# Second network's float64 weights: half-size units through a ring of four, paced behind the gate activations

## The chip, the cores and the metric

The kernel runs on one core of one Trainium2 chip. The metric is the device time of one execution in microseconds (us), the median over runs. Engines are named as in the profile: PE (TensorE's matmuls), PEld (its weight loads, which overlap them), DVE (VectorE), ACT (ScalarE), POOL (GpSimd) and SP (the engine whose queue issues nearly all DMAs here).

## What is computed

An attention between 512 tokens and 32 state rows per batch and head, whose output goes through two feed-forward networks. Inputs `x` and `state` are float32; the weights `w_gate`, `w_val`, `w_out`, `w_in2` (`moe2_w_in`) and `w_out2` (`moe2_w_out`) are float64 and are turned into float32 on the chip.

```python
# attention: x (8, 8, 512, 64), state (8, 8, 32, 64)
scores = scale * np.matmul(x, state.transpose(0, 1, 3, 2))      # softmax -> a
xread = np.matmul(a, state)
scores2 = scale * np.matmul(state, x.transpose(0, 1, 3, 2))     # softmax -> a2
sread = np.matmul(a2, x)
x = concat([xread, sread])            # as rows: (4352, 512)
# first network, d_ff 1536
g = x @ w_gate
x = (g * (1 / (1 + np.exp(-g))) * (x @ w_val)) @ w_out
# second network, d_ff 2048
h = x @ w_in
out = (np.maximum(h, 0) + alpha * np.minimum(h, 0)) @ w_out
```

## The kernel before, in words

The first network goes over eight blocks of 512 tokens (one batch each, `blocks[0]` to `blocks[7]`, called blocks 0 to 7 here) and then one of the 256 state rows. Blocks 0 and 1 run together with the conversion of the first network's weights. Blocks 2 to 7 go through `ffn1`, which is a loop over `f` = 0 to 11, slices of 128 of the 1536 hidden columns. In each `f`, PE makes the gate product (six matmuls) and ACT applies Silu to it (`gate`, tile `s`, from bank `g`); PE makes the value product and DVE multiplies the two (`value`, bank `v`); ACT and DVE split the result in a rounded part and a rest (`split`, tile `h`: ACT writes the first, `sub_lo` on DVE the second); and PE projects the slice before, `project(f - 1)`, twelve matmuls into four banks `acc`. At `f` = 0 `finish` ends the block before: its last projection, copies of the four banks to `xo` (two on ACT, two on DVE), and stores to `x2d`.

`slots` holds what else is done in a block, by `f` and one of three places: 0 behind the gate, 1 behind value and split, 2 behind the projection. There stand the products of the state with the weights (`state_times_w`, tiles `sw`, at place 2 of each even `f`), the attention of the next block's batch (`scores` at `f` = 3 and 7, with two PSUM banks `aux` that they share with `state_times_w`), and the preparation of the second network's weights.

That preparation takes the float64 words in units. `Unit.load` is one DMA of 1 MB of words into a tile `raw`; `Unit.act` is two ACT instructions over the tile's high and low words (L267, L268, 128 x 1024 each); `Unit.bits` is two DVE instructions and a POOL addition for one half of the unit, which leave float32 words in `m32`; `uses` hands them to `take`, which puts sums, splits (`sp`) and stores into the list `later`, of which `one_later` does one or two at place 2. `Stream.step` does the acts of unit d every second step, the bits of a half of unit d - 1, and the uses of a half of unit d - 2, and loads one unit ahead. 16 units (8 of `w_in2`, 8 of `w_out2`, in turn) take 8 steps a block, at `f` = 1, 2, 4, 5, 7, 8, 10, 11 of blocks 2 to 6; block 7 only empties `later`.

In this part PE's order is the order of the program. The order on DVE, ACT, POOL and SP is made by a scheduler when the kernel is built, from the program's dependences; `tc.issue_after(i)` tells it to place what is issued under it behind instruction i. Each engine, and SP's queue of DMAs, then takes its instructions strictly in that order: one that waits holds up all behind it. From the block of state rows on the order of all engines is written out by hand.

Of the kernel before, what the change touches and what calls it, by code (L numbers as in the profile page):

```python
# [25 lines left out]
def attention_and_two_ffns(ctx: ExitStack, tc: tile.TileContext, x, state, w_gate, w_val,  # L26
# [7 lines left out]
    P = 128  # L34
# [9 lines left out]
    XT = 2  # L44
    EARLY = 3

    const = ctx.enter_context(tc.tile_pool(name="const", bufs=1))
# [195 lines left out]
    def words(w, r0, r1, c0, c1):  # L243
        return w.bitcast(I32)[r0 * P:r1 * P, 2 * c0:2 * c1].rearrange("(a p) n -> p a n", p=P)

    class Unit:
# [39 lines left out]
        def uses(self, i):  # L286
            if self.take:
                self.take(i, self.m[i].bitcast(F32))

    class Stream:  # L290

# [47 lines left out]

    units1, units2 = [], []  # L340
    for j in range(NJ1):
# [76 lines left out]
    def one_later():  # L418
        for _ in range(2 if len(later) > 3 else 1):
            if later:  # L420
                later.pop(0)()

    for j in range(NJ2):
        units2.append(Unit([words(w_in2, 0, NPAIR, 2 * P * j, 2 * P * (j + 1))], take=take_w2(j)))
        units2.append(Unit([words(w_out2, 2 * j, 2 * j + 2, 0, DM)], take=take_wo2(j)))
    stream1, stream2 = Stream(units1, 3), Stream(units2, 1)

# [31 lines left out]
    class Block:  # L459
# [21 lines left out]
        def gate(self, f, idle=0):  # L481

            if self.keep:
                if f % 2 == 0:
                    self.kept = t4([P, 2, S], F32, "p")
                self.p[f] = self.kept[:, f % 2]
            else:
                self.p[f] = t2([P, S], F32, "s")[:, :self.n]
            return nc.scalar.activation(self.p[f], self.product(f, 0, self.banks(f)[0], idle), AF.Silu)

# [61 lines left out]
    with tc.manual_schedule(engines={mybir.EngineType.PE}):  # L552
# [67 lines left out]
        def ffn1_slots(b):  # L620
            slots = {}

            def put(f, i, th):
                slots.setdefault((f, i), []).append(th)

            for j in range(1, NJ1):
                put(2 * j - 2, 2, lambda j=j: state_times_w(b, j))
            if b < B - 1:
                for f in range(NF1):
                    if f % 3 != 0:  # L630
                        put(f, 1, stream2.step)
                    put(f, 2, one_later)
            if b == B - 1:
                for f in range(NF1):
                    put(f, 2, one_later)
                put(0, 2, lambda: nc.sync.dma_start(alpha_sb, alpha.rearrange("(k p) -> p k", p=P)))
# [110 lines left out]
        todo.setdefault((1, 10), []).append(lambda: state_times_w(XT, 0))  # L747
        todo.setdefault((1, 8), []).append(lambda: stream2.load(1))
        for b in range(XT):
# [517 lines left out]
```

## Time and profile before

| | us |
|---|---|
| median of 3 runs | 1426.53 (1426.47 to 1428.33) |
| the profiled execution | 1423.65 |
| its span, from first to last instruction | 1421.6 |
| PE busy | 1366.7 (96%) |
| DVE busy | 1031.0 (73%) |
| ACT busy | 826.8 (58%) |
| POOL busy | 554.9 (39%) |

The span has three parts: blocks 0 and 1 with the first weights (up to 203 us), blocks 2 to 7 (203 to 685 us), and the state rows and the second network (from 685 us). PE is the engine to look at: where another engine is idle and PE is not, nothing is lost. Idle time of PE, and time in which its clock is granted at half speed, is what the span can lose.

### The profile page before, as it was taken

What the parts mean: (1) busy time and instruction counts of PE and PEld (TensorE: products, weight loads), DVE (VectorE), ACT (ScalarE), POOL (GpSimd) and SP (SyncE); (2) the same over time, 40 slices, a digit from 0 to 9 for tenths busy, and PEclk for the clock granted to TensorE, in tenths of its full rate; (3) what the DMA queues carried; (4) which work ended last, traced back from release to release, by engine and by line L of the source; (5) the groups of instructions that cost most, each with busy time, mean ns of one, the idle gap of its engine ahead of it and who ended that gap; (6) DMA issues with size and microseconds to landing.
All of it is one profiled execution on the core that took longest, in us unless ns stands there. A gap on an engine that the chain in (4) does not pass through costs nothing.

```text
span 1421.6 us, 20610 instructions
## 1 busy us (share of the span) xinstructions
PE 1366.7 (96%) x7238; PEld 1069.2 (75%) x7238; DVE 1031.0 (73%) x1593; ACT 826.8 (58%) x1408; POOL 554.9 (39%) x422
## 2 busy tenths in 40 slices
PE   6899999989899999999999999999999999999997
PEld 3566777767676676777887888878888888888886
DVE  6878545769687887634566688888897899878651
ACT  6666443565555554433456767666677667666642
POOL 4432111313232332100005665666665656656611
PEclk8999999999999999999999999999999999999999
DMA  9442232495857856310415688679877897786792
GB/s 298 154 157 46 81 104 49 140 243 175 254 149 224 236 173 182 113 45 1 156 53 206 186 279 282 209 185 317 308 234 222 268 317 244 207 245 233 264 311 102
DMA packets 274223, 271.91 MB, mean 191 GB/s; under 512 B 133704, under 2 KB 198216, under 8 KB 273096
## 3 DMA queue, kind: packets, MB, share of 16 engines
q1 hardware_dynamic: 271976, 270.21, 61.6%
q8 instruction: 57, 0.93, 0.3%
q10 hardware_dynamic: 2144, 0.39, 0.2%
q14 instruction: 46, 0.38, 0.1%
HBM read 206.05 MB, written 64.49 MB: 190 GB/s over the span
## 4 chain that ended last, share of the span: by engine, by line
PE 75%; DVE 9%; DMA 5%; ACT 3%; issue 3%; POOL 2%; SPq 2%; ACTq 0%; DVEq 0%; POOLq 0%
PE acc L1036 17%; PE acc L516 16%; PE v L476 8%; PE g L476 8%; PE v L924 7%; PE g L924 5%; PE aux L924 5%; PE aux L442 3%; DVE h L83 2%; DMA raw<-in_moe_w_out_dram 2%; PE acc L1106 2%; DMA wo<-ws2d 1%; DVE sw L83 1%; POOL u L936 1%; PE aux L162 1%
## 5 line engine op out<-in xcount | busy, mean ns | idle before, releaser
L1036 PE MATMUL acc<-h,wo 128*128 128x512 f32 x1344 | 341.5, 390 | 2.5 <-ACT sum L77 1.3
L516 PE MATMUL acc<-h,wp 128*128 128x512 f32 (+1 forms) x1296 | 300.2, 382 | 11.1 <-DVE h L83 8.2
L1036 PEld LDWEIGHTS acc<-h,wo 128*128 128x128 f32 x1344 | 251.2, 188 | 56.4 <-ACT sum L77 2.6
L516 PEld LDWEIGHTS acc<-h,wp 128*128 128x128 f32 x1296 | 235.6, 190 | 63.2 <-DVE h L83 10.6
L893 POOL TENSOR_TENSOR u<-u,m 128x512 f32<-128x512 f32 x96 | 128.6, 1340 | 346.1 <-ACT m L892 312.9
L83 DVE TENSOR_TENSOR h<-u,h 128x512 fp32r<-128x512 f32 x160 | 147.4, 937 | 23.1 <-ACT h L77 22.7
L476 PE MATMUL g<-a,sw 128*128 128x512 f32 x576 | 153.8, 401 | 3.6 <-ACT h L77 1.7
L476 PE MATMUL v<-a,sw 128*128 128x512 f32 x576 | 153.3, 402 | 0.5 <-DVE p L492 0.4
L77 ACT ACTIVATE h<-u 128x512 fp32r<-128x512 f32 x160 | 100.3, 630 | 88.4 <-POOL u L936 87.1
L476 PEld LDWEIGHTS g<-a,sw 128*128 128x128 f32 x576 | 103.8, 188 | 62.6 <-issue 24.3
L924 PE MATMUL v<-x,w 128*128 128x512 f32 x576 | 146.4, 389 | 0.1
L1047 DVE TENSOR_TENSOR sum<-acc,sum 128x512 f32<-128x512 f32 x184 | 125.5, 683 | 24.8 <-PE acc L1036 24.4
L476 PEld LDWEIGHTS v<-a,sw 128*128 128x128 f32 x576 | 106.4, 190 | 33.8 <-issue 9.5
L924 PEld LDWEIGHTS v<-x,w 128*128 128x128 f32 x576 | 107.8, 188 | 22.6 <-DVE u L932 0.5
L284 POOL TENSOR_TENSOR m<-m,raw 128x512 int32<-128x512 int32 x44 | 61.8, 1407 | 153.9 <-DVE m L276 95.5
L83 DVE TENSOR_TENSOR h<-h,h 128x512 fp32r<-128x512 f32 (+1 forms) x80 | 78.7, 984 | 43.1 <-ACT h L77 42.3
L936 POOL TENSOR_TENSOR u<-u,u 128x512 f32<-128x512 f32 x64 | 105.4, 1647 | 5.0
L83 DVE TENSOR_TENSOR sw<-aux,sw 128x512 fp32r<-128x512 f32 x96 | 62.6, 682 | 56.1 <-ACT sw L77 56.1
L77 ACT ACTIVATE h<-s 128x512 fp32r<-128x512 f32 (+1 forms) x84 | 50.3, 598 | 90.5 <-DVE s L492 90.2
L492 DVE TENSOR_TENSOR s<-s,v 128x512 f32<-128x512 f32 (+1 forms) x79 | 52.0, 659 | 67.9 <-PE v L476 54.3
L892 ACT ACTIVATE m<-m,alpha_sb 128x512 f32<-128x512 f32 (+1 forms) x144 | 99.2, 689 | 0.0
L924 PE MATMUL g<-x,w 128*128 128x512 f32 x384 | 97.6, 390 | 0.8 <-ACT h L891 0.8
(155 smaller groups left out, 2120.9 us busy)
## 6 DMA issues: line engine op xcount, KB each, us to landing
wo<-ws2d SPq DMA_DIRECT2D x224, 256.0 KB, 5.2
w<-w2d SPq DMA_DIRECT2D x104, 512.0 KB, 5.5
w2d<-sp SPq DMA_DIRECT2D x32, 512.0 KB, 3.9
raw<-in_moe_w_out_dram SPq DMA_DIRECT2D x14, 1024.0 KB, 5.2
x2r<-x2d SPq DMA_DIRECT2D x25, 512.0 KB, 6.2
w<-w2d SPq DMA_DIRECT2D x48, 256.0 KB, 5.5
x2d<-xo SPq DMA_DIRECT2D x32, 256.0 KB, 3.0
raw<-in_moe_w_in_dram SPq DMA_DIRECT2D x8, 1024.0 KB, 6.2
```

Source lines behind the costliest of these rows:

```text
L77: return nc.scalar.activation(o, i, AF.Copy)
L83: (eng or nc.vector).tensor_tensor(out=o, in0=src, in1=hi.bitcast(F32), op=ALU.subtract)
L284: nc.gpsimd.tensor_tensor(out=m, in0=m, in1=lo, op=ALU.add)
L476: nc.tensor.matmul(o[:, :self.n], self.lhs(f, k, a, which), self.rhs(k, c), start=(i == 0), stop=(i == last))
L492: return nc.vector.tensor_tensor(out=self.p[f], in0=self.p[f], in1=self.product(f, 1, self.banks(f)[1]), op=ALU.mult)
L516: nc.tensor.matmul(self.acc[e][:, :self.n], wo1[f // 2][:, f % 2, a, e * P:(e + 1) * P], t[:, c, :self.n], start=(self.n == S and f == 0 a ...
L892: nc.scalar.activation(n, n, AF.Copy, scale=alpha_sb[:, f:f + 1])
L893: nc.gpsimd.tensor_tensor(out=out, in0=out, in1=n, op=ALU.add)
L924: nc.tensor.matmul(o, w[:, a, q], x[k][:, q, e], start=start and n == 0, stop=stop and n == 5, skip_group_check=True)
L936: nc.gpsimd.tensor_tensor(out=o, in0=x0, in1=x1, op=ALU.subtract)
L1036: nc.tensor.matmul(o, w[:, f, a, e], h[:, q], start=first and i == 0, stop=i == 5, skip_group_check=True)
L1047: nc.vector.tensor_tensor(out=r, in0=o, in1=r, op=ALU.add)
```

## The change

The 16 units of the second network become 32 halves. Each half has a DMA of 0.5 MB of its own, into a quarter of two fixed `raw` tiles (a ring of four, the half `n` takes place `n` mod 4), and two acts of 128 x 512. A step does the acts of half k, the bits of half k - 1 and the uses of half k - 2, and loads half k + 2, which takes the place of half k - 2. There are six steps a block, at `f` = 1, 2, 5, 6, 9, 10, now over blocks 2 to 7. A step stands under `tc.issue_after` of the block's newest gate activation. What the acts, bits and uses compute is as before.

```diff
+    STEPS2 = (1, 2, 5, 6, 9, 10)
...
+    class Half:
+        ring = []
+
+        def __init__(self, src, n, take):
+            self.src, self.n, self.take = src, n, take
+
+        def load(self):
+            if len(Half.ring) < 2:
+                Half.ring.append(t8([P, 2 * HALF, 2], I32, "raw"))
+            self.raw = Half.ring[self.n // 2 % 2][:, HALF * (self.n % 2):HALF * (self.n % 2 + 1)]
+            nc.sync.dma_start(self.raw.rearrange("p (a n) t -> p a (n t)", a=self.src.shape[1]), self.src)
+
+        def act(self):
+            lo, hi = self.raw[:, :, 0], self.raw[:, :, 1]
+            nc.scalar.activation(hi.bitcast(F32), hi.bitcast(F32), AF.Copy, scale=REBIAS)
+            nc.scalar.activation(lo, lo.bitcast(U32), AF.Copy, scale=2.0 ** -29)
+
+        def bits(self):
+            m = self.m = t2([P, HALF], I32, "m32")
...
+            nc.gpsimd.tensor_tensor(out=m, in0=m, in1=lo, op=ALU.add)
+
+        def uses(self):
+            self.take(self.n % 2, self.m.bitcast(F32))
+
+    class Halves:
...
+        def step(self):
+            h = lambda q: [self.halves[q]] if 0 <= q < len(self.halves) else []
+            for u in h(self.k):
+                u.act()
+            for u in h(self.k - 1):
+                u.bits()
+            for u in h(self.k - 2):
+                u.uses()
+            self.k += 1
+            self.load(self.k + 2)
...
-        units2.append(Unit([words(w_in2, 0, NPAIR, 2 * P * j, 2 * P * (j + 1))], take=take_w2(j)))
-        units2.append(Unit([words(w_out2, 2 * j, 2 * j + 2, 0, DM)], take=take_wo2(j)))
-    stream1, stream2 = Stream(units1, 3), Stream(units2, 1)
+        for src, take in ((words(w_in2, 0, NPAIR, 2 * P * j, 2 * P * (j + 1)), take_w2(j)),
+                          (words(w_out2, 2 * j, 2 * j + 2, 0, DM), take_wo2(j))):
+            n = src.shape[1] // 2
+            for i in range(2):
+                halves2.append(Half(src[:, n * i:n * (i + 1)], len(halves2), take))
+    stream1, stream2 = Stream(units1, 3), Halves(halves2)
...
-            return nc.scalar.activation(self.p[f], self.product(f, 0, self.banks(f)[0], idle), AF.Silu)
+            self.gated = nc.scalar.activation(self.p[f], self.product(f, 0, self.banks(f)[0], idle), AF.Silu)
+            return self.gated
...
+            def paced():
+                with tc.issue_after(blocks[b].gated.ins):
+                    stream2.step()
+
             for j in range(1, NJ1):
                 put(2 * j - 2, 2, lambda j=j: state_times_w(b, j))
-            if b < B - 1:
-                for f in range(NF1):
-                    if f % 3 != 0:
-                        put(f, 1, stream2.step)
-                    put(f, 2, one_later)
+            for f in range(NF1):
+                if f in STEPS2:
+                    put(f, 1, paced)
+                put(f, 2, one_later)
             if b == B - 1:
-                for f in range(NF1):
-                    put(f, 2, one_later)
...
-        todo.setdefault((1, 8), []).append(lambda: stream2.load(1))
+        todo.setdefault((1, 8), []).append(lambda: stream2.load(2))
```

PE's order of instructions does not change. On the other engines it changes in blocks 2 to 7 and shortly ahead of them, and nowhere from the block of state rows on. Three places follow; the numbers behind a name are buffers'.

ACT, block 3, from the Silu of `f` = 1 to the `sw` copies behind `f` = 2. Before (`h_2666` is the split of `f` = 0, `h_2731` of `f` = 1, `h_2787` of `f` = 2, `raw_2734` the acts of a unit):

```order
L489 ACTIVATE s_2714<-g_2715 128x512
L77 ACTIVATE h_2666<-s_2626 128x512
L77 ACTIVATE sw_2693<-aux_2694 128x512
L77 ACTIVATE sw_2699<-aux_2700 128x512
L77 ACTIVATE h_2731<-s_2714 128x512
L77 ACTIVATE sp_2758<-sc_2709 128x512 x2
L489 ACTIVATE s_2766<-g_2767 128x512
L77 ACTIVATE h_2787<-s_2766 128x512
L267 ACTIVATE raw_2734<-raw_2734 128x1024
L268 ACTIVATE raw_2734<-raw_2734 128x1024
L77 ACTIVATE sw_2806<-aux_2807 128x512
L77 ACTIVATE sw_2812<-aux_2813 128x512
```

The same stretch after, from the Silu of `f` = 1:

```order
L547 ACTIVATE s_2722<-g_2723 128x512
L307 ACTIVATE raw_1801<-raw_1801 128x512
L308 ACTIVATE raw_1801<-raw_1801 128x512
L78 ACTIVATE h_2739<-s_2722 128x512
L547 ACTIVATE s_2765<-g_2766 128x512
L307 ACTIVATE raw_1801<-raw_1801 128x512
L308 ACTIVATE raw_1801<-raw_1801 128x512
L78 ACTIVATE h_2786<-s_2765 128x512
L78 ACTIVATE sw_2808<-aux_2809 128x512
L78 ACTIVATE sw_2814<-aux_2815 128x512
```

The acts have moved from between split and `sw` to right behind each Silu, ahead of that slice's split, and the split of `f` = 0 no longer stands behind the Silu of `f` = 1.

DVE, block 3, `f` = 0 and 1. Before (`s` is the multiplication of `value`, `s_2626` of `f` = 0 and `s_2714` of `f` = 1; `h_2666` is the rest of the split of `f` = 0):

```order
L492 TENSOR_TENSOR s_2626<-s_2626,v_2658 128x512
L80 COPY xo_2681<-acc_370_1996 128x512
L80 COPY xo_2687<-acc_372_1998 128x512
L492 TENSOR_TENSOR s_2714<-s_2714,v_2723 128x512
L83 TENSOR_TENSOR h_2666<-s_2626,h_2666 128x512
L83 TENSOR_TENSOR sw_2693<-aux_2694,sw_2693 128x512
```

After (`s_2631` and `h_2671` are of `f` = 0, `s_2722` of `f` = 1):

```order
L551 TENSOR_TENSOR s_2631<-s_2631,v_2663 128x512
L84 TENSOR_TENSOR h_2671<-s_2631,h_2671 128x512
L84 TENSOR_TENSOR sw_2698<-aux_2699,sw_2698 128x512
L81 COPY xo_2686<-acc_370_1997 128x512
L81 COPY xo_2692<-acc_372_1999 128x512
L84 TENSOR_TENSOR sw_2704<-aux_2705,sw_2704 128x512
L84 TENSOR_TENSOR sp_2715<-sc_2626,sp_2714 128x512 x2
L551 TENSOR_TENSOR s_2722<-s_2722,v_2731 128x512
```

The split's rest for `f` = 0 now stands right behind its own multiplication and not behind that of `f` = 1.

SP's queue of DMAs at the start of block 3. Before (`raw_2734` is the unit whose acts stand in the first piece above):

```order
L126 DMA xq_2651<-in_x_dram 32x16x32 x4
L139 DMA xn_2656<-in_x_dram 128x4x256
L525 DMA x2d_89<-xo_2681 128x512
L525 DMA x2d_89<-xo_2684 128x512
L525 DMA x2d_89<-xo_2687 128x512
L525 DMA x2d_89<-xo_2690 128x512
L258 DMA raw_2734<-in_moe_w_out_dram 128x2x1024
L407 DMA ws2d_108<-sp_2758 128x4x256
```

After:

```order
L584 DMA x2d_89<-xo_2695 128x512
L461 DMA ws2d_108<-sp_2714 128x4x256
L461 DMA ws2d_108<-sp_2715 128x4x256
L303 DMA raw_1799<-in_moe_w_in_dram 128x2x512
L418 DMA w2d_101<-sp_2829 1024x1x128
L419 DMA w2d_101<-sp_2830 1024x1x128
L303 DMA raw_1801<-in_moe_w_out_dram 128x1024
L140 DMA xn_2912<-in_x_dram 128x4x256
```

The loads still stand behind the stores of the block before, but these two are of halves whose acts come at `f` = 5 and 6, where the 1 MB load was of the unit whose acts come at `f` = 2.

## Rows read from the trace of the kernel before

**Rows 1.** The page's head and busy times: busy us, share of the span, instructions.

```profile
span 1421.6 us, 20610 instructions
PE 1366.7 (96%) x7238; PEld 1069.2 (75%) x7238; DVE 1031.0 (73%) x1593; ACT 826.8 (58%) x1408; POOL 554.9 (39%) x422
```

**Rows 2.** Windows, blocks 2 to 7: stretch, length, busy by engine, clock, DMA, GB/s.

```profile
202.62:280.74 78.12, 78.12 (x466) 56.56 (x465) 50.52 (x96) 37.55 (x63) 19.04 (x16) 1.00 0.31 77
280.74:365.12 84.38, 80.32 (x466) 57.26 (x465) 65.05 (x128) 48.07 (x82) 24.58 (x22) 0.98 0.73 209
365.12:449.32 84.20, 80.40 (x466) 57.61 (x465) 65.58 (x128) 48.12 (x82) 25.24 (x22) 0.98 0.73 209
449.32:531.69 82.37, 78.75 (x466) 56.48 (x464) 64.72 (x124) 48.28 (x82) 24.61 (x22) 1.00 0.73 214
531.69:612.23 80.54, 78.49 (x466) 56.47 (x464) 52.78 (x98) 36.16 (x64) 13.44 (x12) 1.00 0.48 133
612.23:684.79 72.56, 72.56 (x377) 55.20 (x376) 27.78 (x40) 24.10 (x40) 0.00 (x0) 1.00 0.07 22
```

**Rows 3.** Timeline of PE, block 3: start, us, instruction, count [idle before, releaser].

```profile
291.77 2.79 PE L516 MATMUL acc<-h,wp 128*128 128x512 f32 x11 [1.13 <-DVE h L83]
...
305.42 1.61 PE L162 MATMUL aux<-xt,bd 128*64 128x512 f32 x4 [2.82 <-DVE sw L83]
306.96 2.69 PE L476 MATMUL v<-a,sw 128*128 128x512 f32 x6
```

**Rows 4.** Timeline of PE, the same waits in blocks 5 and 6.

```profile
460.35 2.83 PE L516 MATMUL acc<-h,wp 128*128 128x512 f32 x11 [1.13 <-DVE h L83]
...
473.60 1.08 PE L162 MATMUL aux<-xt,bd 128*64 128x512 f32 x4 [2.38 <-DVE sw L83]
...
554.37 1.08 PE L162 MATMUL aux<-xt,bd 128*64 128x512 f32 x4 [0.97 <-DVE sw L83]
```

**Rows 5.** Windows, behind the second wait of block 3, columns as above.

```profile
306.00:308.00 2.00, 2.00 (x7) 0.85 (x4) 2.00 (x4) 0.83 (x3) 1.57 (x2) 0.50 0.45 147
```

**Rows 6.** Timeline of ACT, block 3, ahead of the second wait.

```profile
302.04 1.14 ACT L267 ACTIVATE raw<-raw 128x1024 f32<-128x1024 f32 x1 [2.25 <-DMA raw<-in_moe_w_out_dram]
...
304.06 1.07 ACT L77 ACTIVATE sw<-aux 128x512 fp32r<-128x512 f32 x2
```

**Rows 7.** Timeline of DVE, block 3.

```profile
290.43 0.69 DVE L492 TENSOR_TENSOR s<-s,v 128x512 f32<-128x512 f32 x1 [4.04 <-PE v L476]
291.03 0.68 DVE L83 TENSOR_TENSOR h<-s,h 128x512 fp32r<-128x512 f32 x1
...
304.67 1.29 DVE L83 TENSOR_TENSOR sw<-aux,sw 128x512 fp32r<-128x512 f32 x2 [2.42 <-ACT sw L77]
```

**Rows 8.** SP's timeline in block 3, and landing times of the loads of raw.

```profile
293.87 0.75 SPq L258 DMA_DIRECT2D raw<-in_moe_w_out_dram  x1
...
DMA to landing us min/median/max: 5.0/5.7/8.1
```

**Rows 9.** Timeline of ACT, block 2, splits of f = 1 and 2.

```profile
213.03 0.63 ACT L77 ACTIVATE h<-s 128x512 fp32r<-128x512 f32 x1 [1.19 <-DVE s L492]
...
218.47 0.63 ACT L77 ACTIVATE h<-s 128x512 fp32r<-128x512 f32 x1 [1.49 <-DVE s L492]
```

**Rows 10.** Groups of ACT in blocks 2 to 6: busy, mean ns | idle, releasers.

```profile
L267 ACT ACTIVATE raw<-raw 128x1024 f32<-128x1024 f32 x13 | 14.9, 1144 | 19.0 <-DMA raw<-in_moe_w_out_dram 12.3 <-DMA raw<-in_moe_w_in_dram 5.7 <-POOL sp L83 0.9
L268 ACT ACTIVATE raw<-raw 128x1024 int32<-128x1024 uint32 x13 | 14.5, 1119 | 0.0
...
L77 ACT ACTIVATE sp<-m 128x512 fp32r<-128x512 f32 x16 | 9.1, 617 | 0.0
```

**Rows 11.** Timeline of DVE and of PE, block 2, f = 1 and 2.

```profile
213.70 0.69 DVE L83 TENSOR_TENSOR h<-s,h 128x512 fp32r<-128x512 f32 x1 [0.70 <-ACT h L77]
...
217.48 1.75 PE L516 MATMUL acc<-h,wp 128*128 128x512 f32 x7
```

**Rows 12.** Timeline of PE, behind block 7.

```profile
700.42 1.65 PE L516 MATMUL acc<-h,wp 128*128 128x256 f32 x11 [2.53 <-DVE h L83]
```

More of the change, by code (lines that the diff above doesn't have):

```diff
@@ L288, in uses, with __init__, load @@
                 self.take(i, self.m[i].bitcast(F32))
+    class Half:
[13 more added lines that the diff above has]
+            m = self.m = t2([P, HALF], I32, "m32")
+            lo, hi = self.raw[:, :, 0], self.raw[:, :, 1]
+            nc.vector.tensor_scalar(out=m, in0=hi, scalar1=0x0FFFFFFF, scalar2=3, op0=ALU.bitwise_and,
+                                    op1=ALU.logical_shift_left)
+            nc.vector.scalar_tensor_tensor(out=m, in0=hi, scalar=-0x80000000, in1=m, op0=ALU.bitwise_and,
+                                           op1=ALU.bitwise_or)
+            nc.gpsimd.tensor_tensor(out=m, in0=m, in1=lo, op=ALU.add)
+        def uses(self):
+            self.take(self.n % 2, self.m.bitcast(F32))
+    class Halves:
+        def __init__(self, halves):
+            self.halves, self.k, self.loaded = halves, 0, 0
+        def load(self, n):
+            while self.loaded < min(n, len(self.halves)):
+                self.halves[self.loaded].load()
+                self.loaded += 1
+        def step(self):
[8 more added lines that the diff above has]
+            self.load(self.k + 2)
     class Stream:
@@ L338, in unit_o @@
                     banks=("acc0", "acc1") if j < EARLY else ("g", "v"))
-    units1, units2 = [], []
+    units1 = []
     for j in range(NJ1):
@@ L421, in one_later @@
                 later.pop(0)()
+    halves2 = []
     for j in range(NJ2):
-        units2.append(Unit([words(w_in2, 0, NPAIR, 2 * P * j, 2 * P * (j + 1))], take=take_w2(j)))
-        units2.append(Unit([words(w_out2, 2 * j, 2 * j + 2, 0, DM)], take=take_wo2(j)))
-    stream1, stream2 = Stream(units1, 3), Stream(units2, 1)
+        for src, take in ((words(w_in2, 0, NPAIR, 2 * P * j, 2 * P * (j + 1)), take_w2(j)),
[4 more added lines that the diff above has]
+    stream1, stream2 = Stream(units1, 3), Halves(halves2)
     class StateTimesW:
```

## The prediction

> **What bounds the kernel now.** I read the page's busy times first: PE is busy for 1366.7 us of a span of 1421.6 [rows 1], so a change can only give back PE's idle time and time at a lower clock. The windows by block come next. Blocks 2 to 6 have the same PE work, 466 matmuls each, yet block 2 takes 78.12 us with PE busy throughout, and blocks 3, 4, 5 and 6 take 84.38, 84.20, 82.37 and 80.54 [rows 2]. So block 2 shows what a block costs when nothing holds PE up, and the four others lie 6.26, 6.08, 4.25 and 2.42 us above it, 19.01 us together. PE's idle time in them (length less PE busy) is 4.06, 3.80, 3.62 and 2.05, 13.53 us together; the other 5.48 us is PE time that got longer.
>
> PE's timeline tells where. In block 3 PE waits twice: 1.13 us in the projection of f = 0 for DVE's `h` (line 83), and 2.82 us ahead of `scores` at f = 3 for DVE's `sw` [rows 3]. The same two stand in blocks 4 and 5, and block 6 still waits 0.97 us for `sw` at `scores` [rows 4]. Behind the 2.82 us the granted clock is 0.50 of full speed, 1.2 GHz in place of 2.4, in the window from 306 to 308 us [rows 5], and six matmuls of `v` take 2.69 us there [rows 3]. That is where most of the longer PE time of blocks 3 and 4 comes from, whose mean clock is 0.98 against 1.00 in the other blocks [rows 2].
>
> The timelines of the other engines tell why. At f = 3 `scores` needs a PSUM bank that `sw` holds until ACT and DVE have read it. ACT comes to `sw` at 304.06 only, because the acts of a unit stand ahead of it in ACT's order and wait 2.25 us for their DMA [rows 6]; DVE then waits 2.42 us for ACT [rows 7]. The load was issued at 293.87, behind the block's stores in SP's queue, and landings took up to 8.1 us [rows 8]. At f = 1 it is order alone: DVE writes the rest of `h` of f = 0 at 291.03, behind the multiplication of f = 1, which waited until 290.43 for PE's `v` [rows 7]; in ACT's order, too, that split stands behind the Silu of f = 1.
>
> **The change part by part.** PE's work and order are the same, so each part is a question of whether it leaves PE without a wait.
>
> The f = 1 wait. The new order has the rest of `h` of f = 0 right behind its own multiplication, as in block 2, where PE did not wait. The wait goes in blocks 3 to 6.
>
> The f = 3 wait. Three things go at once. No act stands any more between the split of f = 2 and `sw`; the acts at f = 1 and 2 are of halves that were loaded at f = 9 and 10 of the block before; and a load at f = 1 now serves f = 5. A slice of f is about 78.12 / 12 = 6.5 us, so a load has at least three slices, 19.5 us, and mostly four, 26 us. A whole unit landed within 5.0 to 8.1 us [rows 8]; half of it should not take longer. The ACT waits for raw, 12.3 + 5.7 us in blocks 2 to 6 [rows 10], should be near 0.
>
> What is added on ACT. 32 halves with two acts each take the place of 16 units with two of 1144 and 1119 ns [rows 10], 36.2 us. A 128x512 act costs between half of these, 0.57 us, and the 617 ns of another copy of that shape [rows 10]; I take 0.6 us, so 38.4 us, 2.2 us more on an engine that is busy for 47 to 57% of these blocks. What matters is their place, between the Silu and the split. There ACT sat idle for 1.19 and 1.49 us in block 2, waiting for DVE [rows 9]. Two acts fill 1.14 to 1.23 us of that, so a split is late by 0.04 us at most where the data is there. The cover behind that is wide: in block 2 the rest of `h` of f = 1 started at 213.70 and PE began to project that slice at 217.48 [rows 11], 3.1 us after the 0.69 us of DVE's instruction. I cost it at 0. If that cover were gone, each us of lateness would be a us of PE.
>
> What is added on DVE, POOL and SP. The same bits, additions and stores, over six blocks in place of five. DVE is busy for 65 of 84 us in block 3 [rows 2] and gets six halves a block in place of eight. Behind the split of f = 2 it has its bits and four small sums ahead of `sw`, so `sw` there can still be late by DVE alone. The bounds for that are 0, as in block 2, and the 0.97 us of block 6 [rows 4] in each of four blocks, 3.9 us; I take 1 us in all, near block 2, since the work ahead of it shrinks. Each SP load now waits for the POOL addition of the half whose place it takes, which belongs to the step before; stores and loads for attention are queued behind it, with slices of time left, so 0.
>
> Block 7 had no steps and 27.78 us of DVE and 24.10 us of ACT in 72.56 [rows 2]. It gets four with acts and the list behind them. There an early weight split for the state rows on ACT, placed in front of the split of f = 5, now waits for the last half's POOL addition to free its buffer. I count about 1 us for that wait and a cover of about 2 us until the projection of f = 5: 0, at worst one wait like the 2.53 us behind block 7 [rows 12].
>
> Behind block 7 all orders are as before, and the wait there, on a reload of the first blocks' results, stays.
>
> **The sum.** 1423.65 us (profiled execution) - 19.01 (blocks 3 to 6 down to block 2) + 1 (left of f = 3) = 1405.6 us. The median of the runs, 1426.53, is 1.002 of the profiled execution, so 1405.6 becomes 1408.5 us.
>
> The Trainium skill speaks against the smaller loads: its page "DMA: Bandwidth & Descriptors", section Measured, says to batch DMAs to 1 MiB or more, and its section on the anatomy of one DMA puts a fixed 2.0 us on each. By that an estimate from the page is 16 x 2.0 = 32 us of DMA time more, and no run here has shown a half yet. Were that exposed in full, the sum would be 1440 us; it is not by the lead above.
>
> **The rivals.** First, loads that come late after all. If a half isn't there when its act comes, ACT stands with the split and `sw` behind it, and PE pays what block 3 paid at f = 3: 6.26 less about 1.5 for the f = 1 wait with its restart, about 4.7 us. There are 15 pairs of acts behind the first pair. Five such pairs cost 23.5 us and make it slower than before; all cost 70, 1423.65 - 19 + 70 = 1475 us, 1478 as a median. For it: SP's loads wait for POOL, and SP is in order. Against it: 19.5 us and more of lead for 8.1 at most. This is the place where the page's rule would bite. Chance 7%.
>
> Second, a smaller gain: the waits shrink but stay. DVE as the last to come at `scores` would leave 0.97 us in each of four blocks, and if the restart or a reordered `h` at f = 1 leaves 1.5 us each, 4 x 2.5 = 10 us stays; a new wait in block 7 would be about 4 us with half a clock period behind it. Gain 8 to 15 us, 1411.5 to 1418.5. For it: block 6 shows a wait for `sw` although no acts stand there any more (the 16 units' are done by the end of block 5), and the new order puts DVE's sums ahead of `sw`. Against it: block 2 has the same engines and no wait. Chance 20%.
>
> Third, no change: the waits go to other places of the same blocks, for instance to the projections, since a split stands behind two acts in every paced slice. That needs 17 us of new waits, 0.5 us in each of 34 steps. Against it: the cover of 3.1 us [rows 11]. Chance 6%. That the change doesn't do what it says can be left out, since the new orders stand in front of the reader.
>
> **How the numbers follow.** The forecast, 1408.5 us (1405 to 1411.5), has 67%; smaller gain 20%; no change 6%; slower 7%. The range reaches from 1405, which is all of the 19.01 and 2.5 us more, to 1418, nearly the end of the smaller gain, and leaves out the 13% of the last two and some edges. A measurement of this kernel can tell about 0.2% (2.9 us) from no change. Faster by more than that 0.87, within it 0.06, slower 0.07.
>
> **What would show it.** Right: blocks 3 to 6 at about 78 us each; no PE wait for `h` at f = 1 and under 1 us for `sw` at f = 3; granted clock 1.00 through blocks 2 to 7; ACT's waits for the DMA of raw gone; block 7 still near 72.6 us. Wrong: ACT waits for raw in front of a split, or PE waits at projections of f = 2, 3, 6, 7, 10 and 11, or a block 7 above 75 us.

## The result, and the profile after

The changed kernel's median is 1406.67 us (1405.95 to 1407.7 over 4 runs), that of the kernel before on the same chip 1427.32 us, a ratio of 0.9856 [0.9839, 0.9873]. The forecast was 1408.5 us. The profiled execution took 1406.81 us, 16.84 less than that of before; the sum in the prediction, ahead of its scaling to the median, ended at 1405.6. All medians of before below are from the chip of the run named, so ratios are to be compared and not medians.

The page of after, span and first busy row, against [rows 1]:

```profile
span 1405.0 us, 20644 instructions
PE 1361.7 (97%) x7238; PEld 1066.8 (76%) x7238; DVE 1037.8 (74%) x1593; ACT 827.5 (59%) x1440; POOL 556.7 (40%) x422
```

PE busy time fell by 5.0 us and the span by 16.6, so PE lost 11.6 us of waiting. Blocks 2 to 7 in windows from one block's first gate product to the next's (length, then busy time and instruction count of PE, PEld, DVE, ACT and POOL, the granted clock, the DMA share and GB/s), against [rows 2]:

```profile
203.63:281.81 78.18, 78.18 (x466) 56.57 (x464) 51.45 (x97) 42.01 (x73) 17.18 (x15) 1.00 0.44 118
281.81:360.41 78.60, 78.30 (x466) 56.50 (x464) 60.24 (x118) 43.90 (x80) 20.80 (x18) 1.00 0.64 174
360.41:438.86 78.45, 78.15 (x466) 56.49 (x465) 59.25 (x110) 43.95 (x80) 21.36 (x18) 1.00 0.68 184
438.86:517.41 78.55, 78.25 (x465) 56.50 (x464) 59.42 (x114) 43.91 (x80) 20.38 (x18) 1.00 0.63 173
517.41:595.89 78.48, 78.18 (x465) 56.53 (x464) 57.42 (x105) 43.75 (x80) 21.04 (x18) 1.00 0.64 176
595.89:668.45 72.56, 72.56 (x378) 55.23 (x376) 42.23 (x69) 31.49 (x58) 7.77 (x7) 1.00 0.33 106
```

Blocks 3 to 6 take 314.08 us together where they took 331.49: -17.41. The start of block 2 is 1.01 us later, block 2 itself 0.06 longer, block 7 the same, and what follows it 0.26 shorter; that is the span. Each of blocks 3 to 6 is within 0.5 us of block 2, with the clock at 1.00, and PE waits once in each, 0.30 us for `sw`: in blocks 3 and 5 at f = 3, in the place of the 2.82 and 2.38 of [rows 3, 4], in blocks 4 and 6 at the second `scores`, f = 7. PE's timeline, block 3, f = 2 to f = 3 (start, duration, then in brackets the wait ahead and its releaser):

```profile
300.50 1.66 PE L534 MATMUL g<-a,sw 128*128 128x512 f32 x6
302.45 1.08 PE L163 MATMUL aux<-xt,bd 128*64 128x512 f32 x4 [0.30 <-DVE sw L84]
303.46 1.66 PE L534 MATMUL v<-a,sw 128*128 128x512 f32 x6
```

Six matmuls of `v` take 1.66 us there, against 2.69 in [rows 3]. ACT's timeline of the same block, from the split of f = 0 on, shows both causes gone (against [rows 6, 9]): that split stands ahead of the Silu of f = 1, the acts of a half run between a Silu and its split without a wait for a DMA, and nothing stands between the split of f = 2 and `sw`, which waits for PE alone.

```profile
285.52 0.63 ACT L78 ACTIVATE h<-s 128x512 fp32r<-128x512 f32 x1 [1.55 <-DVE s L551]
...
291.48 0.62 ACT L547 ACTIVATE s<-g 128x512 f32<-128x512 f32 x1
291.96 0.71 ACT L307 ACTIVATE raw<-raw 128x512 f32<-128x512 f32 x1
292.51 0.71 ACT L308 ACTIVATE raw<-raw 128x512 int32<-128x512 uint32 x1
293.47 0.63 ACT L78 ACTIVATE h<-s 128x512 fp32r<-128x512 f32 x1 [0.24 <-DVE s L551]
...
297.66 0.63 ACT L78 ACTIVATE h<-s 128x512 fp32r<-128x512 f32 x1 [0.46 <-DVE s L551]
300.61 1.09 ACT L78 ACTIVATE sw<-aux 128x512 fp32r<-128x512 f32 x2 [2.32 <-PE aux L500]
```

The tile `raw` in blocks 2 to 7 (count, ns minimum/median/maximum, first and last start, forms; last the us from a DMA's issue to its landing), against [rows 8, 10]:

```profile
L307 ACT ACTIVATE raw<-raw x32: 648/672/708, 212.7 to 610.1; 128x512 f32<-128x512 f32 x32
L308 ACT ACTIVATE raw<-raw x32: 647/670/713, 213.2 to 610.7; 128x512 int32<-128x512 uint32 x32
...
DMA to landing us min/median/max: 3.6/4.2/5.9
```

### The profile page after: what moved, and what is told of

Read it like the earlier page. It is cut to its first block, busy times and chain, and to the rows that moved or that the text cites. A ratio compares the mean times of both kernels' runs of the same rounds, so it can differ in the third digit from the quotient of the medians.

```text
span 1405.0 us, 20644 instructions
## 1 busy us (share of the span) xinstructions
PE 1361.7 (97%) x7238; PEld 1066.8 (76%) x7238; DVE 1037.8 (74%) x1593; ACT 827.5 (59%) x1440; POOL 556.7 (40%) x422
## 4 chain that ended last, share of the span: by engine, by line
PE 79%; DVE 7%; POOL 4%; issue 3%; ACT 3%; DMA 3%; SPq 0%; POOLq 0%; DVEq 0%; ACTq 0%
PE acc L1096 17%; PE acc L575 17%; PE g L534 9%; PE v L534 9%; PE v L984 7%; PE aux L984 5%; PE g L984 5%; PE aux L500 3%; POOL u L996 2%; PE acc L1166 2%; DVE h L84 1%; POOL u L953 1%; PE aux L163 1%; PE aux L223 1%; DMA wo<-ws2d 1%
## 5 line engine op out<-in xcount | busy, mean ns | idle before, releaser
L84 DVE TENSOR_TENSOR h<-u,h 128x512 fp32r<-128x512 f32 x160 | 151.6, 964 | 24.1 <-ACT h L78 23.8
L317 POOL TENSOR_TENSOR m<-m,raw 128x512 int32<-128x512 int32 x32 | 46.3, 1447 | 156.4 <-DVE m L315 115.7
L78 ACT ACTIVATE sw<-aux 128x512 fp32r<-128x512 f32 x96 | 52.6, 595 | 86.6 <-PE aux L500 79.3
L984 PE MATMUL aux<-x,w 128*128 128x512 f32 x384 | 97.6, 390 | 0.0
```

The lines of the kernel that those rows point to most:

```text
L78: return nc.scalar.activation(o, i, AF.Copy)
L84: (eng or nc.vector).tensor_tensor(out=o, in0=src, in1=hi.bitcast(F32), op=ALU.subtract)
L317: nc.gpsimd.tensor_tensor(out=m, in0=m, in1=lo, op=ALU.add)
L984: nc.tensor.matmul(o, w[:, a, q], x[k][:, q, e], start=start and n == 0, stop=stop and n == 5, skip_group_check=True)
```

## The experiments

The change has three parts: halves (with their ring), the spread over six blocks, and the pacing behind the gate activations. The first six runs put them together in other ways. Theory A in their expectations is the theory of order: ACT takes its instructions strictly in order, so a Silu or the acts of `raw` that stand ahead of an older slice's split, or of the `sw` copies, make PE wait, and the pacing takes that away. The runs bent it more than once.

**The pacing alone** (before, and):

```diff
+            def paced():
+                with tc.issue_after(blocks[b].gated.ins):
+                    stream2.step()
...
-                    if f % 3 != 0:
-                        put(f, 1, stream2.step)
...
+                if b < B - 1 and f % 3 != 0:
+                    put(f, 1, paced)
```

> The kernel before with one part of the change: steps of whole 1 MB units, eight a block over blocks 2 to 6 as before, but each step is placed behind the block's newest gate activation. Theory A (order: a block waits where acts stand ahead of the sw copies of f = 2, and where the split of f = 0 stands behind the Silu of f = 1): here ACT's order at f = 3 is free of acts, but the split of f = 0 still stands behind the Silu of f = 1 and now behind two acts too, so the wait at f = 3 goes and the one at f = 1 grows to 2 to 3.5 us; 8 to 12 us less than before, about 1417 us. Theory B (each of pacing, halves and spreading brings its share): a third of the 20 us, about 1420 us. Theory C (loads: what counts is how early the load of a unit is issued before its acts): no load moves much, so at most 3 us less than before, about 1425 us.

Measured: 0.9965 [0.9951, 0.9978], about 5 us. Blocks 3 to 5 take 82.65, 81.52 and 82.44. PE's waits for `sw` at f = 3 are gone from these blocks but for 0.30 us in block 4, and that at f = 1 grew from 1.13 us [rows 3] to 1.82 and 0.28 in block 3, with eleven matmuls of 4.31 us behind it in place of 2.79:

```profile
292.96 0.50 PE L517 MATMUL acc<-h,wp 128*128 128x512 f32 x1 [1.82 <-ACT h L77]
293.74 4.31 PE L517 MATMUL acc<-h,wp 128*128 128x512 f32 x11 [0.28 <-DVE h L83]
```

There the acts of a whole unit (1.09 and 1.10 us) stand with the Silu of f = 1 ahead of the split of f = 0. The direction was right, the size half of what was expected.

**The spread alone** (whole units, the six steps of `STEPS2` in blocks 2 to 6, six in block 7; `paced` is the bare step here):

```diff
-                    if f % 3 != 0:
-                        put(f, 1, stream2.step)
+                if f in (STEPS2 if b < B - 1 else (1, 2, 4, 5, 7, 8)):
+                    put(f, 1, paced)
```

> The kernel before with one part of the change: whole 1 MB units and no placing behind the gate, but six steps a block over blocks 2 to 7 (at f = 1, 2, 5, 6, 9, 10, in block 7 at 1, 2, 4, 5, 7, 8). Theory A (order): the scheduler's order has no acts ahead of the sw copies of f = 2 and the split of f = 0 ahead of the Silu of f = 1, so blocks 3 to 6 come to 78 to 79.5 us each, 1407 to 1412 us. Theory B (shares): about 1420 us. Theory C (loads): units still come one unit ahead, the waits at f = 3 shrink only where a step is farther from its load; 1415 to 1421 us.

Measured: 0.9979 [0.9966, 0.9993], a miss for theory A. Block 3 fell to 81.01, block 4 rose to 85.85, and block 7 to 74.31. In block 4 acts that wait 2.97 us for their DMA stand ahead of `sw`, `sp` and the copies of the banks (`xo`), and PE's projection waits for the banks. PE, and ACT:

```profile
375.15 5.46 PE L517 MATMUL acc<-h,wp 128*128 128x512 f32 x12 [3.68 <-DVE xo L81]
```

```profile
369.21 1.15 ACT L268 ACTIVATE raw<-raw 128x1024 f32<-128x1024 f32 x1 [2.97 <-DMA raw<-in_moe_w_out_dram]
370.25 1.10 ACT L269 ACTIVATE raw<-raw 128x1024 int32<-128x1024 uint32 x1
...
373.25 1.06 ACT L78 ACTIVATE xo<-acc 128x512 f32<-128x512 f32 x2
```

**The halves alone** (after without the pacing, eight steps in five blocks):

```diff
-                with tc.issue_after(blocks[b].gated.ins):
-                    stream2.step()
+                stream2.step()
...
-                if f in STEPS2:
+                if b < B - 1 and f % 3 != 0:
```

> The changed kernel with one part of the change only: halves through the ring of four, loaded two ahead, but eight steps a block at the old places over blocks 2 to 6 and no placing behind the gate. Theory A (order): no acts stand between the split of f = 2 and sw, and the split of f = 0 stands ahead of the Silu of f = 1, so 1407 to 1413 us. Theory B (shares): about 1420 us. Theory C (loads): a load is two steps ahead of its acts and the waits for the DMA go, 1407 to 1411 us; the f = 1 wait, which is no matter of loads, stays at 1.1 us a block.

Measured: 0.9962 [0.9951, 0.9973], a miss for theories A and C. Blocks 3 to 5 take 82.46, 81.12 and 82.60, block 2 rises to 81.11, and block 6, then without steps, takes 78.10. The waits are at f = 5 now, where a transpose needs the bank that `sw` of f = 4 holds. ACT has the Silu of f = 5 first, which waits for its gate product, and the split and `sw` of f = 4 behind it. PE, and ACT:

```profile
320.08 1.13 PE L213 MATMUL aux<-ident,e 128*128 128x128 f32 x4 [2.53 <-DVE sw L84]
```

```profile
317.59 0.60 ACT L547 ACTIVATE s<-g 128x512 f32<-128x512 f32 x1 [3.76 <-PE g L534]
318.08 0.62 ACT L78 ACTIVATE h<-s 128x512 fp32r<-128x512 f32 x1
318.60 1.08 ACT L78 ACTIVATE sw<-aux 128x512 fp32r<-128x512 f32 x2
```

**Pacing and spread with whole units** (the second kernel with the pacing of the first):

```diff
-                stream2.step()
+                with tc.issue_after(blocks[b].gated.ins):
+                    stream2.step()
```

> The kernel before with two parts of the change: six steps a block over six blocks (in block 7 at f = 1, 2, 4, 5, 7, 8), each behind the newest gate activation, but with whole 1 MB units and acts of 128 x 1024. Theory A (order): splits and sw stand as in the changed kernel, two acts of 1.1 us each in front of a split delay it by about 1 us, which the 3.1 us of cover hide; 1407 to 1411 us. Theory B (shares): about 1413.5 us. Theory C (loads): the whole units are loaded one unit ahead, two steps, so like the spread-only kernel, 1415 to 1421 us.

Measured: 1.0016 [1.0002, 1.0029], no gain at all from two parts that gain 0.3% and 0.2% alone. Theory B, that each part brings its share, had come nearest for each part by itself (about 1420 us expected, 1418 to 1422 measured) and fails here with theory A: 1413.5 us expected, 1426.39 measured. Blocks 3 and 5 take 79.0, blocks 4 and 6 take 86.85 and 87.33, and there the same order stands at f = 5 with a whole unit's acts in it:

```profile
402.87 0.86 PE L213 MATMUL aux<-ident,e 128*128 128x128 f32 x4 [4.56 <-DVE sw L84]
```

**The change without the pacing:**

```diff
-                with tc.issue_after(blocks[b].gated.ins):
-                    stream2.step()
+                stream2.step()
```

> The changed kernel without one part: its steps are not placed behind the gate activation (halves, ring of four, six steps over six blocks stay). The kernels with one or two parts showed that parts do not add. Theory A, mended (a block waits where the scheduler's order puts the Silu of the next slice, or acts whose load has not landed, ahead of a slice's split, sw or bank copies): this order has no Silu ahead of an older split in any block, and loads come two steps ahead, so 1407 to 1412 us on a chip where the kernel before takes 1427 us, a ratio of 0.986 to 0.991. Theory D (it takes the placing behind the gate to keep the acts away from where PE waits): some blocks pay 2 to 4 us, as with the other kernels without it, ratio 0.995 or above.

Measured: 0.9878 [0.9849, 0.9907], blocks 3 to 6 at 78.70, 78.47, 78.66 and 78.53, with four waits of 0.30 us as in after. With halves and spread the scheduler puts no Silu ahead of an older split by itself, and the pacing adds nothing to the time that these runs can tell. ACT does wait for `raw`'s DMA here, ten times for 0.52 to 2.18 us, and none of PE's waits stands behind one of these.

**The change over five blocks:**

```diff
-                if f in STEPS2:
+                if b < B - 1 and f % 3 != 0:
```

> The changed kernel without one part: eight steps a block over blocks 2 to 6 in place of six over blocks 2 to 7 (halves, ring of four and the placing behind the gate stay). Theory A, mended: in blocks 3 to 6 at least three times ACT's order has the Silu of f = 5 and two pairs of acts ahead of the split and the sw copies of f = 4, the order that cost 4.56 us and a clock period in the kernel with pacing and spreading; three to four times 5 to 7 us go back, ratio 0.994 to 1.000. Theory D (the placing behind the gate is what helps): ratio 0.986 to 0.990, as in the changed kernel.

Measured: 0.9988 [0.9976, 1.0]. Halves and pacing stay, the spread goes, and with it the gain: blocks 3 to 5 take 83.89, 84.73 and 85.03. ACT's order at f = 4 and 5 is Silu, acts, Silu, acts, and then the split and `sw` of f = 4:

```profile
317.81 0.78 PE L213 MATMUL aux<-ident,e 128*128 128x128 f32 x4 [3.61 <-DVE sw L84]
```

**The load two steps later** (after; a half is loaded in the very step that does its acts, not two steps ahead of it):

```diff
+            self.load(self.k + 1)
             self.k += 1
-            self.load(self.k + 2)
```

> The changed kernel with each half loaded in the very step that does its acts, no longer two steps ahead; ACT's order of instructions is the same as in the changed kernel. Measures the price of a late load, the prediction's first rival. That rival's price is 4.7 us for each pair of paced slices: 16 pairs, 75 us more than the changed kernel, about 1480 us. Counted by slices: the load lands 4 to 6 us after the Silu, the split is then late by 4 to 5 us against a cover of 3.1 us, and sw of f = 2 and 6 by 2 to 3 us against a cover near 1 us; 3 us a pair and some clock periods, 45 to 60 us more, about 1460 us. If loads do not matter at this order, no change from 1407 us.

Measured: 0.986 [0.9835, 0.9885], as after. This did not test what it was for. The scheduler put the loads of block 3 at 294.77, 303.67, 323.87 and 330.87 us; in after they stand at 296.30, 305.20, 325.41 and 332.42, and the whole block starts 1.54 us later there. A load goes where its place in the ring comes free, wherever the program names it.

**The split of f = 0 put behind the Silu of f = 1** (after, blocks 2 to 7):

```diff
+            if f == 1 and blk.n == S:
+                with tc.issue_after(blk.gated.ins):
+                    blk.split(0)
...
-            if blk.n == S:
+            if blk.n == S and f:
```

> The changed kernel with one thing put back: in blocks 2 to 7 the split of f = 0 stands behind the Silu of f = 1 on ACT, as in blocks 3 to 5 of the kernel before. Theory A: PE waits in the projection of f = 0 for 1.1 to 2.5 us in each of six blocks, with 0.4 us of restart each, 9 to 17 us more than the changed kernel, ratio to the kernel before 0.992 to 0.998. If that place is hidden otherwise (bank copies or DVE's order set the time there), no change, ratio 0.986.

Measured: 1.0009 [0.9998, 1.002]. One displaced split a block gives back the whole gain, more than was expected. It is a little more than one instruction: the scheduler moved DVE's rest of the split with it, and in blocks 4 and 6, which pay most, this rest stands behind the multiplication of f = 1 too (at 375.73 us behind 375.13 in block 4). Blocks 2 to 7 take 79.22, 80.30, 85.00, 81.90, 83.60 and 73.84. PE in block 4:

```profile
374.36 0.49 PE L575 MATMUL acc<-h,wp 128*128 128x512 f32 x1 [1.48 <-ACT h L78]
376.46 5.06 PE L575 MATMUL acc<-h,wp 128*128 128x512 f32 x11 [1.61 <-DVE h L84]
```

The two waits are 3.1 us together, and then eleven matmuls take 5.06 us, where twelve take 2.88 at full clock. That the order can cost this much was shown; that it was this order which cost the kernel before its time was not, and two of the next runs were made for that, one for the late load.

**A ring of two** (after, with one `raw` tile for two halves):

```diff
-            if len(Half.ring) < 2:
+            if len(Half.ring) < 1:
...
-            self.raw = Half.ring[self.n // 2 % 2][:, HALF * (self.n % 2):HALF * (self.n % 2 + 1)]
+            self.raw = Half.ring[0][:, HALF * (self.n % 2):HALF * (self.n % 2 + 1)]
...
-            self.load(self.k + 2)
+            self.load(self.k + 1)
```

> The kernel after with a ring of two places in place of four: half n takes place n mod 2, so its load has to wait for the POOL addition of half n - 2 and comes one step ahead of its acts, where the kernel after has it two steps ahead. This is the price of the first rival, which the run with the load in its own step did not test, because the load's place in SP's order hardly moved there. The scheduler now orders the acts behind the split in about half of the steps, and in two of the six blocks a Silu stands ahead of an older split. Rival (a late load costs 4.7 us for each pair of acts): 31 pairs, of which those that wait behind a split cost less; more than 25 us over the kernel after, so a ratio to the kernel before of 1.004 or more. Order theory (what counts is which older split or bank copy stands behind the waiting instruction): the acts behind a split hold up sw and the next Silu only, so the blocks with the displaced Silu pay 3 to 5 us each and the others under 2; 8 to 18 us over the kernel after, 0.991 to 0.998. If loads have so much lead that even one step is enough: 0.986 as the kernel after, and ACT shows no wait for raw's DMA.

Measured: 0.9943 [0.9927, 0.9959], inside the range of the order theory and far from the rival's 1.004: blocks 2, 3 and 5 take 78.22, 78.68 and 78.64, blocks 4 and 6 take 84.40 and 83.17. Seven times ACT waits for `raw`'s DMA, 0.37 to 2.54 us, in every block once or twice, and no PE wait stands behind any of them. The two long blocks are those with a Silu ahead of an older split, at f = 5 again:

```profile
395.22 1.13 PE L213 MATMUL aux<-ident,e 128*128 128x128 f32 x4 [3.61 <-DVE sw L84]
```

```profile
349.59 0.68 ACT L307 ACTIVATE raw<-raw 128x512 f32<-128x512 f32 x1 [1.81 <-DMA raw<-in_moe_w_out_dram]
...
391.65 0.60 ACT L547 ACTIVATE s<-g 128x512 f32<-128x512 f32 x1 [5.32 <-PE g L534]
```

So these late loads had no price of their own, like those of the change without the pacing. What a late load costs depends on what stands behind its acts: in the kernel before it was `sw`, in block 4 of the spread alone `sw` and the bank copies.

**The split first** (before, each Silu behind the split of the slice ahead of it, nothing else):

```diff
-            blk.gate(f)
+            if f and blk.n == S:
+                with tc.issue_after(blk.cut.ins):
+                    blk.gate(f)
+            else:
+                blk.gate(f)
...
-            acopy(t[:, 0, :self.n], p)
+            self.cut = acopy(t[:, 0, :self.n], p)
```

> The kernel before with one thing changed: the Silu of a slice is placed behind the split of the slice ahead of it, in ACT's order. That undoes the one displacement of the kernel before (in blocks 3, 4 and 5 the Silu of f = 1 stood ahead of the split of f = 0), and leaves units, 8 steps a block and the acts ahead of sw at f = 3 as they are. Order theory: the f = 1 wait of 1.1 to 1.8 us goes in these blocks, the f = 3 wait of 2.8 us and the half-clock stretch behind it stay; 3 to 6 us less than before, 0.996 to 0.998. If both waits hang together by the clock or by what comes next: more than 8 us less, under 0.994. If DVE's order (the rest of h behind the next multiplication) is what counted and not ACT's: no change, 1.000.

Measured: 1.0024 [1.0015, 1.0033], slower by a little, where the order theory wanted 3 to 6 us less. The wait at f = 1 is gone, as told, and that at f = 3 has grown to 4.84, 4.05 and 4.24 us (2.82, 2.56 and 2.38 before). Blocks 3 to 5 take 84.87, 84.80 and 85.04: the first two 0.5 and 0.6 us longer than before, block 5 2.67 longer, with a granted clock of 0.96 where it was 1.00. PE, ACT and SP of block 3, against [rows 3, 6, 8]:

```profile
306.25 1.90 PE L162 MATMUL aux<-xt,bd 128*64 128x512 f32 x4 [4.84 <-DVE sw L83]
```

```profile
302.90 1.10 ACT L267 ACTIVATE raw<-raw 128x1024 f32<-128x1024 f32 x1 [3.19 <-DMA raw<-in_moe_w_out_dram]
303.90 1.08 ACT L268 ACTIVATE raw<-raw 128x1024 int32<-128x1024 uint32 x1
304.89 1.06 ACT L77 ACTIVATE sw<-aux 128x512 fp32r<-128x512 f32 x2
```

```profile
286.02 5.82 SPq L126 DMA_DIRECT2D xq<-in_x_dram  x8
...
292.47 2.35 SPq L525 DMA_DIRECT2D x2d<-xo  x4
294.91 1.28 SPq L258 DMA_DIRECT2D raw<-in_moe_w_out_dram  x1
```

In blocks 3 to 5 of the kernel before one chain holds the end: SP comes to the load behind the loads of `xq` and the stores of `xo`, the load lands 8 us later, the acts and `sw` follow, and PE goes on. It ends when it ends: counted from the block's start, PE goes on at 25.19, 24.40 and 24.58 us here and at 24.68, 24.46 and 24.28 in the kernel before. What PE no longer waits at f = 1 it waits at f = 3.

**Pacing and the split first together** (before, with both edits of order, whole units, five blocks):

```diff
+                with tc.issue_after(blocks[b].gated.ins):
+                    stream2.step()
...
+                with tc.issue_after(blk.cut.ins):
+                    blk.gate(f)
```

> The kernel before with its units, eight steps a block and five blocks, and two changes of order alone: each step stands under issue_after of the newest gate activation (as in the run with the pacing alone), and each Silu stands behind the split of the slice ahead of it (as in the run with the split first). The first took the wait for sw at f = 3 and left 1.82 us at f = 1; the second took the wait at f = 1 and left 4.84 us at f = 3, where ACT stood for a load with sw behind it. Order theory: each of the two orders feeds one of two chains to PE (split to projection of f = 0; load, acts, sw to scores), and only both together take the excess of blocks 3 to 5: 79 us each or less, a ratio to the kernel before of 0.985 to 0.990, like the kernel after without halves and without the sixth block. Rival (the eight steps of whole units are too much for these blocks, halves and the sixth block are what pays): a wait comes up elsewhere in the same blocks, as in all five-block runs so far, 81 us or more, 0.994 to 1.000.

Measured: 0.9933 [0.9919, 0.9946], about 9.5 us: between the 0.985 to 0.990 of the one theory and the 0.994 to 1.000 of the other, nearer the other. Two edits that bring -0.35% and +0.24% alone bring -0.67% together, so the two orders do feed two chains, and the acts' place is the one that binds first. Blocks 3 to 6 take 82.11, 79.47, 80.40 and 80.50. PE still waits for `sw`, 0.97 to 2.06 us, now with DVE as the late one, and block 3 restarts at a lower clock. PE, DVE and POOL in block 3:

```profile
301.02 1.70 PE L162 MATMUL aux<-xt,bd 128*64 128x512 f32 x4 [2.06 <-DVE sw L83]
302.65 2.62 PE L476 MATMUL v<-a,sw 128*128 128x512 f32 x6
```

```profile
298.58 1.38 DVE L355 TENSOR_TENSOR sc<-sc,m 128x128 f32<-128x128 f32 x1
...
300.29 1.28 DVE L83 TENSOR_TENSOR sw<-aux,sw 128x512 fp32r<-128x512 f32 x2
```

```profile
298.20 1.61 POOL L284 TENSOR_TENSOR m<-m,raw 128x512 int32<-128x512 int32 x1 [5.03 <-DVE m L276]
```

So order alone is worth about half of the gain with whole units, and halves with the sixth block give the rest, and the order as well, as the run without the pacing shows. Over all kernels, a Silu ahead of an older split stands in ACT's order in blocks 3 to 5 of before, of the pacing alone, the halves alone and the five blocks, in blocks 4 and 6 of the pacing with the spread and of the ring of two, in all six blocks of the displaced split, and in none of after or of the change without the pacing. Each of these blocks is at least 1 us longer than the same block of after. The reverse does not hold: the blocks of the spread alone, of the split first and of this run are longer without it, by acts, by a load's chain and by DVE.

**The reloads behind block 7 issued first** (after, the four reloads `x2r` of the first blocks' results, of which the expectation says two, ahead of block 7's stores in SP's queue):

```diff
-                slots.setdefault((1 + i // 2, 2), []).append(th)
+                slots.setdefault((1 + i // 2, 2) if i else (0, 0), []).append(th)
```

> The kernel after with the first two reloads of the first blocks' results (x2r from x2d, for the second network's first tiles) issued at place 0 of f = 0 in the block of state rows in place of place 2 of f = 1, so ahead of block 7's four stores in SP's queue. A try for a version that beats both kernels: the wait of 3.16 us behind block 7 hangs on them in the kernel after. If that chain is right: 2 to 4 us less than the kernel after, a ratio to the kernel before of 0.983 to 0.985. If the wait has another releaser: the same as the kernel after, 0.986.

Measured: 1403.18 us, 0.9853 [0.9837, 0.9869]. In the trace the wait of 3.16 us is gone, and from the state rows to the end it takes 733.32 us in place of 736.55. After, and then this kernel, at the same matmuls:

```profile
684.70 1.58 PE L575 MATMUL acc<-h,wp 128*128 128x256 f32 x11 [3.16 <-DVE h L84]
```

```profile
680.29 1.60 PE L575 MATMUL acc<-h,wp 128*128 128x256 f32 x12
```

That chain is shown. That the kernel as a whole is faster than after is not: the two ratios overlap nearly in full, and the two were not run on one chip together.

## Why the prediction was right, point by point

**What bounds the kernel.** Right: blocks 3 to 6 could come down to block 2, and did, to within 0.33 to 0.48 us each.

**The f = 1 wait.** It went, as forecast, but not with a price of its own. The prediction put about 1.5 us of block 3's 6.26 on it and left 4.7 to the late load; the run with the split first takes that wait away alone, and the block gets longer, 84.87 us. In the kernel before the load's chain held all of the 6.26, and the f = 1 wait lay in its shade. Only where that chain is short does the split's order show: waits of 1.82 us with the pacing alone, up to 6.5 us a block in the run with the split put behind. In block 6 there was no such wait to take: PE's wait at that place, 1.09 us of the block's 2.42, was for the bank copies `xo`, which DVE made behind four sums. The prediction names only the 0.97 us for `sw` in that block and counts all of the 2.42 as gain. The wait did go, since in after `xo` follows the first `sw` directly (in block 6 at 525.32 us, 7.9 us from its start where it was 9.8), but no step of the prediction says why, so that 1 us was luck. PE, then DVE, in block 6 of before:

```profile
542.36 3.01 PE L516 MATMUL acc<-h,wp 128*128 128x512 f32 x12 [1.09 <-DVE xo L80]
```

```profile
541.52 1.28 DVE L80 COPY xo<-acc 128x512 f32<-128x512 f32 x2
```

**The f = 3 wait.** Right in cause and size: 1 us was to be left in all, 1.20 is (four times 0.30, two of them at f = 7). The late one is DVE, as forecast, though not by load: `sc` takes 1.39 us in place of 0.28 while POOL adds (below).

**The added acts.** The step that was mis-sized: 0.6 us each, with bounds of 0.57 and 0.617, and the rows show 0.67. It cost nothing, since two of them start 0.55 us apart and the split behind them still waits 0.24 us for DVE; the 3.1 us of cover were not needed in that place. (By [rows 2] ACT was busy for 45 to 59% of blocks 2 to 6, not for 47 to 57; nothing rests on it.)

**DVE, POOL, SP and block 7.** Apart from the four times 0.30 us none of it cost time: block 7 takes 72.56 us as before. The text on the change says that a whole step is held behind the gate activation. The traces show that this holds for ACT's instructions alone: in block 3 the bits of the step at f = 2 start at 293.35 us, ahead of that slice's Silu at 295.51, and with the load in its own step the loads stood where they had been. The forecast didn't rest on it.

**Behind block 7.** The wait was to stay at 2.53 us, and is 3.16, but no restart at half clock follows it now: 736.55 us from the state rows on, against 736.81.

**The sum.** Forecast -18.0 us, measured -16.84. The four blocks gave 17.41 where 18.0 was forecast. Block 2 starts 1.01 us later, which no step names and whose cause was not looked for. The rest of the difference is +0.06 in block 2, -0.26 behind block 7 and -0.24 outside the span. The scaling to the median, 1.002, added 2.9 us that this kernel does not show (its median lies 0.1 us below its profiled execution); the two errors partly cancel.

**The rivals.** Late loads: no act of a half waits for its DMA in after. The price of 4.7 us a pair was wrong as well, as the ring of two shows: seven late pairs, none with a PE wait behind it. The smaller gain came only in kernels with a part missing. Halves land in 3.6/4.2/5.9 us (minimum, median, maximum) where whole units took 5.0/5.7/8.1 [rows 8], so by the medians two halves take 8.4 us where a unit took 5.7; smaller loads do cost more, but none is waited for. The Trainium skill, "DMA: Bandwidth & Descriptors", section Measured, says to batch DMAs to 1 MiB or more, from loads that GpSimd issued; these are issued by SP. The rows agree that a smaller load pays more for its bytes, and show that this is no loss where the load has lead enough.

**What the chances left out.** That the parts do not add. Of halves, spread and pacing, any one alone gives 0.2 to 0.4%, pacing with either of the others 0.1% or nothing, halves with spread all of it, within the error. The change without the pacing has no act between the split of f = 2 and `sw` of block 3 either: with halves and spread the pacing was not needed for that.

## What to carry to other kernels

Where each engine's order is fixed when the kernel is built, read for each wait which older instruction stands behind the one that waits, and look at the order again after every change: a scheduler moves a Silu or a copy by one place, and that place cost 1 to 6.5 us a block here. Two waits in one block may be one chain; take away the earlier alone and see whether the later one grows before you price both. Make pieces small enough to fit an engine's gaps, and ask of each load not only whether it is late but what stands behind the instruction that waits for it.

## What the runs showed of the hardware

**DVE stands still beside a POOL addition.** In the kernel after, a 128x128 sum that takes 0.28 us elsewhere takes 1.39 while POOL adds two tiles; it ends 0.15 us after POOL. DVE, and POOL:

```profile
299.88 0.28 DVE L409 TENSOR_TENSOR sc<-m 128x128 f32<-128x128 f32 x1
300.08 1.39 DVE L409 TENSOR_TENSOR sc<-sc,m 128x128 f32<-128x128 f32 x1
301.50 0.29 DVE L409 TENSOR_TENSOR sc<-m,sc 128x128 f32<-128x128 f32 x1
```

```profile
299.98 1.34 POOL L317 TENSOR_TENSOR m<-m,raw 128x512 int32<-128x512 int32 x1 [3.70 <-issue]
```

The rows of the pacing with the split first show the same (1.38 us beside POOL's 1.61). Without these 1.1 us DVE could begin `sw` when ACT's first copy of it ends, at about 301.20 us by the rows (two copies from 300.61 on, 0.59 each) in place of 301.71. That is an estimate of 0.5 us, enough for the 0.30 us that are left; it was not tried. The Trainium skill has the rule, "SBUF — State Buffer", section Who interferes with whom: a DVE instruction with two SBUF inputs contends with a GpSimd instruction that reads SBUF, the port pair that they share is an exclusive lock, and the order of issue decides who is blocked. The rows agree: the POOL addition began 0.10 us ahead of the sum.

**The clock after a wait.** In these traces TensorE's granted clock often falls to half behind a wait, not always, and the wait's length alone does not tell. Two windows of two us: one from 0.7 us behind the end of the 2.53 us wait in block 3 of the halves alone (clock 0.50, the 1.2 GHz level), one from the end of the 3.16 us wait in after (1.00, the 2.4 GHz level):

```profile
320.80:322.80 2.00, 2.00 (x7) 1.61 (x7) 2.00 (x5) 1.04 (x2) 0.00 (x0) 0.50 0.60 194
```

```profile
684.70:686.70 2.00, 2.00 (x16) 2.00 (x17) 2.00 (x3) 0.42 (x1) 0.00 (x0) 1.00 1.01 356
```

What decides between them stays open.
